# Query loads by one iteration instead of two, and weights issued 600 KB further ahead

## The chip, the cores and the metric

The kernel runs on one core of a Trainium2 chip. The metric is the device time of one execution in microseconds (us). Before the change three runs took 405.43, 406.85 and 407.35 us, median 406.85.

The engines of the core work side by side, each through its own list of instructions in order: TensorE (PE, with its weight loads as PEld), VectorE (DVE), ScalarE (ACT), GpSimd (POOL) and SyncE (SP). They wait for one another through semaphores. SP does nothing here but issue DMA loads and stores, in the order in which the program wrote them; an issue that has to wait holds up all that come after it.

## The reference, cut to what matters

Three steps follow one another: a local attention with global tokens, a soft mixture of experts, and a feed-forward layer.

```
s_g   = scale * q_g @ k_all^T;  out_g = softmax(s_g) @ v_all          # 32 global queries see all keys
s_ll  = where(|i - j| <= 32, scale * q_l @ k_l^T, -1e9)               # 512 local queries: a band
s_lg  = scale * q_l @ k_g^T                                           # and the 32 global keys
out_l = softmax([s_lg, s_ll]) @ [v_g, v_l]
x     = [out_g, out_l], heads side by side                            # 2176 tokens x 512

logits = x @ phi;  d = softmax over tokens;  slots = d^T @ x          # 8 experts x 4 slots
out_e  = relu(slots_e @ w1_e) @ w2_e;  y = softmax over slots(logits) @ out

h = y @ w_in;  g = h - tanh(h);  result = g @ w_out
```

There are 4 batches of 8 heads with 512 local and 32 global positions of 64 numbers, all float32. w1 and w2 are 8 x 512 x 1024 and 8 x 1024 x 512; w_in is 512 x 2048, w_out 2048 x 512. The expert weights are the largest part of the bytes, 33.5 MB.

## The kernel before, in words

**The attention loop** (line 664) makes 33 iterations, `it` = 0 to 32. The 32 pairs of batch and head are taken four at a time, which gives eight *stages* `s`; a stage has four *groups* of queries, `t` = 0 to 3, and iteration `it` = 4s + t scores group `it`. One iteration does several things, each for another group:

- `local_scores(it)` (line 236): PE multiplies the queries with their window of keys (L248), VectorE masks and takes maxima (L254), ScalarE takes the exponentials (L258).
- POOL then prepares the next group: `roll_k(it)` shifts the window of keys in place, and `spread_q(it + 1)` (line 138) copies the next group's queries into `q_b[2]`, the only buffer that the score matmuls read. So this copy waits for the scores of group `it`, and the scores of the next group wait for this copy.
- `local_transpose(it - 1)` (L269), `local_values(it - 2)` (L281) and `global_values(it - 2)` (L475) finish older groups; `roll_v(it - 2)` shifts the values on POOL.
- When `it` % 4 = 2, `global_probs` takes the scores of the next stage's global queries with all of its keys (L430). When t = 1, `spread_k(s + 1)` copies the next stage's global keys beside its local ones, on POOL; when t = 3, `spread_v(s + 1)` does so with global values. In the profile all POOL copies stand at line 210, and are told apart by their tiles: q, k, v, and k<-qg for `spread_k`.

**Where SP's loads come from.** All loads go through `load` (line 98), which adds their KB to the counter `queued` and issues them on SP; in the profile they stand at line 104. In the loop an iteration issues, in this order: queries (in even iterations), the next stage's values (`load_v`, first part with the global values `vg` when t = 2, second part when t = 3), then weights, and, when t = 3, the global queries and keys (`qg`) and the local keys of the stage after the next (`load_qk(s + 2)`).

Queries lie in two buffers `q_b[0]` and `q_b[1]` of 256 KB, each for two groups; group g stands in half g % 2 of buffer (g // 2) % 2. `load_q(h)` in iteration `it` = 2h - 4 fills both halves of buffer h % 2, for groups it + 4 and it + 5. The groups that stood there were it and it + 1, and the last reader of these is `spread_q(it + 1)`, in the same iteration. So SP waits with this load for that copy on POOL.

Weights have no fixed place. The `while` loop of line 724 issues them as long as the KB issued so far are under a pace:

```
while queued < LEAD + PACE * it:
    if len(raw_t) < min(NIN, (it - C0 + 3) // 2 + 1) and free:
        load_raw()
    elif not len(free) > (KEEP if len(raw_t) < NIN else 0) or not load_w():
        break
```

`load_raw` brings 512 KB of w_in as raw words in two loads of 256 KB (`in_w_in`); eight of these are converted during the loop. `load_w` brings one 512 KB piece of w1 or w2 (`in_w`). Both take a slot of 29; a raw slot comes back after its conversion, a weight's slot only when the experts have used it. With LEAD = 2700 and PACE = 1200 the loop may be 2,700 KB ahead of 1,200 KB an iteration. Near the end of the loop, from iteration 27, buffers of the attention are turned into more slots.

**After the loop** come the mixture's slots, the experts (from some 140 us; L971 and L1010), and the feed-forward layer (L1133 and L1174 to L1176), which fills the rest of the time from some 180 us.

Of the kernel before, what the change touches and what calls it, by code (L numbers as in the profile page):

```python
# [18 lines left out]
NT = 17  # L19
NE = 8  # L20
WARM = 3
LEAD, PACE = 2700, 1200
KEEP = 2
SPK = 1
C0 = 4
# [37 lines left out]
def band_attention_soft_moe_tanhshrink_kernel(  # L63
# [34 lines left out]
    def load(out, in_):  # L98
        nonlocal queued
        n = 8 if in_.dtype == mybir.dt.int64 else 4  # L100
        for _, c in out.ap:
            n *= c
        queued += n >> 10
        DMA.dma_start(out=out, in_=in_)  # L104
# [18 lines left out]
    def spread_k(s):  # L123
        kg = qg_t[s][:, 128:192].rearrange("p (i c) -> p i c", i=2)
        pcopy(k_t[s][:, :, 3], kg[:, :, None].to_broadcast([128, 2, 6, 32]))

    def spread_v(s):
        v = v_t[s][96:128]
        pcopy(v[:, 1:6], v[:, 0:1].to_broadcast([32, 5, 260]))


    def load_q(h, cols=slice(0, 256)):
        load(
            out=q_b[h % 2].rearrange("p (a t) -> p a t", a=2)[:, :, cols],
            in_=qd[h // 2][:, :, 256 * (h % 2) + cols.start:256 * (h % 2) + cols.stop],
        )

    def spread_q(g, copies):
        for par in range(2):
            r = slice(64 * par, 64 * par + 64)  # L140
            copies[par](
                q_b[2][r].rearrange("p (a b t) -> p a b t", a=2, b=2)[:, :, par],
                q_b[g // 2 % 2][r].rearrange("p (a h t) -> p a h t", a=2, h=2)[:, :, g % 2],
            )
# [42 lines left out]
    def selectors():  # L187
        V.tensor_reduce(out=istk, in_=ident.rearrange("p (g s) -> p s g", g=4), op=ALU.add, axis=AX.X)
# [13 lines left out]
    NG = 4 * NST  # L202
# [15 lines left out]
    def roll_k(g):  # L218
        k = k_t[g // 4]
        for a, b, q in ROLLS[g % 4]:  # L220
            pcopy(k[:, :, q, a:b], k[:, :, q, a + 1:b + 1])

    def roll_v(g):
        v = v_t[g // 4]
        for a, b, q in ROLLS[g % 4]:
            r = slice(32 * q, 32 * q + 32)
            if g < NG - 2:
                pcopy(v[r, a:b], v[r, a + 1:b + 1])
            else:
                pcopy(v[r, a:b, 0:130], v[r, a + 1:b + 1, 0:130])  # L230
                S.copy(*(v[r, i:i + b - a, 130:260] for i in (a, a + 1)))
# [4 lines left out]
    def local_scores(g, fill):  # L236
        s, t = divmod(g, 4)
        k = k_t[s]
        sm = wk.tile([128, 512], F32, tag="sm", name="sm").rearrange("p (j c) -> p j c", j=4)
        mb = wk.tile([128, 4], F32, tag="mb", name="mb")  # L240
        for f in fill[0:1]:
            f()
        for h2 in range(2):
            sc = psS.tile([128, 2, 128], F32, tag="S", name="sc", padded_shape=[128, 2, 256])
            for a in range(2):
                jj = 2 * h2 + a
                for i in range(2):
                    T.matmul(  # L248
                        sc[64 * i:64 * i + 64, a, :], lhsT=q_b[2][:, 256 * i + jj:256 * i + 256:4],
                        rhs=k[:, i, :, WINDOWS[t][jj][0]], skip_group_check=True, tile_position=(0, 64 * i),  # L250
                    )
            for a in range(2):
                jj = 2 * h2 + a
                V.tensor_tensor_reduce(  # L254
                    out=sm[:, jj, :], in0=sc[:, a, :], in1=mask[WINDOWS[t][jj][1]],
                    scale=-0.125, scalar=3e38, op0=ALU.add, op1=ALU.min, accum_out=mb[:, jj:jj + 1],
                )
                S.activation(  # L258
                    out=sm[:, jj, :], in_=sm[:, jj, :], func=AF.Exp, scale=-1.0, bias=mb[:, jj:jj + 1]
                )  # L260
            for f in fill[1 + h2:2 + h2]:
                f()
        sm_t[g] = sm

    def local_transpose(g):
        p = sm_t.pop(g)
        ps = psT.tile([128, 512], F32, tag="T", name="ptp")
        for u in range(4):
            T.transpose(ps[:, 128 * u:128 * u + 128], p[:, u, :], ident)  # L269
        pt = wk.tile([128, 512], F32, tag="pt", name="pt")  # L270
        S.copy(out=pt, in_=ps)
        pt_t[g] = pt
# [342 lines left out]
    def win_head(c):  # L615
        f32_head(win[c].bitcast(I32), raw_t[c][0])

    def win_ops(c):
        return f32_tail(win[c].bitcast(I32), *raw_t[c])
# [5 lines left out]
    def open_chains():  # L625
        for c in chains:
            if c[0][0]:
                c[0][0]()

    def step_chains():  # L630
        for c in chains:
            if c[0][1]:
                c[0][1]()
        chains[:] = [c[1:] for c in chains if len(c) > 1]
# [5 lines left out]
    with tc.manual_schedule():  # L640
# [23 lines left out]
        for it in range(NG + 1):  # L664
            s, t = divmod(it, 4)
            open_chains()
            last = fill[3:]
            if it < NG:
                local_scores(it, fill)
                if it:  # L670
                    roll_k(it)
                    if it < NG - 1:
                        spread_q(it + 1, (pcopy, pcopy))
            if 1 <= it < NG + 1:
                local_transpose(it - 1)
            free.extend(cool)
            cool.clear()
            if it < NG and it >= C0 and (it - C0) % 2 == 0 and (it - C0) // 2 < NIN:
                win_head((it - C0) // 2)
                fill = win_ops((it - C0) // 2)  # L680
            else:
                fill = []
            if it >= 2:
                local_values(it - 2)
                global_values(it - 2)
                roll_v(it - 2)
            for f in last:
                f()
            step_chains()
            gs = (it + 2) // 4 if it % 4 == 2 and it + 2 < NG else 0 if it == 0 else None  # L690
            if gs is not None:
                c = global_probs(gs)
                c[0][1]()
                if it == 0:
                    spread_q(1, (pcopy, pcopy))
                    roll_k(0)

                chains.append([(c[1][0], c[2][1])] + c[3:] if gs == 0 else c[1:])
            if it == 4:
                selectors()  # L700
            if it % 8 == 7:
                chains.append(global_turn(it // 8))
            i = it - 2
            if i >= 0 and (i // 4) % 2 == 1:
                chains.append(turn_x(4 * (i // 8) + i % 4))
            if it in (11, 19, 27):
                chains.append(dispatch((it - 11) // 8)[0])
            if it < NG and t == SPK and s < NST - 1:
                spread_k(s + 1)
            if it == 0:  # L710
                spread_v(0)
            if it < NG and t == 3 and s < NST - 1:
                spread_v(s + 1)
            if it % 2 == 0 and it < NG - 4:
                load_q(it // 2 + 2)
            if it < NG:
                if it == NG - 5:
                    phi_g = ap_.tile([128, 192], F32, tag="qg", name="phi_g", bufs=1)
                    phi_g = phi_g[:, 0:128].rearrange("p (k s) -> p k s", k=4)
                    load(out=phi_g, in_=phid[1])  # L720
                if t in (2, 3) and 1 <= s < NST - 1:
                    load_v(s + 1, t - 2)
# [6 lines that stand above are left out]
            if it < NG and t == 3 and s + 2 < NST:  # L729
                load_qk(s + 2)  # L730
            if it == NG - 5 or it == NG - 1:
                reuse(ap_.tile([128, 1536], F32, tag="k", name="k_w"))
            if it == NG - 3:
                reuse(ap_.tile([128, 1560], F32, tag="v", name="v_w"))
            if it == NG - 2:
                free.append((wk, "x", 1024, 3))
            if NG - 3 <= it < NG:
                reuse(q_b[it - NG + 3])
            if it == NG - 3:
                reuse(pg[:, 0, 0:512])  # L740
            if it == NG - 1:
                reuse(pg.rearrange("p a c -> p (a c)")[:, 512:1536])
# [676 lines left out]
    with tc.If(small < 1):  # L1419
        for t0, nt in [(0, 4), (4, 2), (6, 4), (10, 2), (12, 3), (15, 2)]:  # L1420
            steps[:] = [(t0, nt, fc, fc == 0, fc == 15) for fc in range(16)]
            for i in range(18):
                if i < 16:
# [3 lines left out]
                    u, g = (r[:, i % 2, 0:n] for r in (u_r, g_r))  # L1427
# [76 lines left out]
```

## Time and profile before

| | us |
|---|---|
| median of 3 runs | 406.85 (405.43 to 407.35) |
| profiled execution, its own time | 406.85 |
| its span, first to last instruction | 405.1 |
| PE busy | 382.9 |
| DVE busy | 276.2 |
| ACT busy | 218.2 |
| POOL busy | 209.7 |

The span is the time between the first and the last instruction; the execution's own time is 1.75 us longer. The profile's page gives each engine's busy time and cuts the span into 40 slices, each with a digit for its busy tenths. Further views list waits (who waited for whom, and how long), give the busy time of stretches, show a timeline of one engine, and list each DMA issue with its KB and the time from its issue to the landing of its last byte. "issue" as the releaser means that the profile shows nothing that was waited for. `sc`, `gsc` and `X` are the tiles of the local scores, the global scores and the local values.

### The profile page before, as it was taken

To read this page: it belongs to the slowest core of one execution; us is meant where nothing else is said; L and a number is where in the kernel's file an instruction comes from. 1 tells how busy PE (TensorE), PEld (TensorE's weight loads), DVE (VectorE), ACT (ScalarE), POOL (GpSimd) and SP (SyncE) were. 2 spreads that over 40 slices of the span, in tenths; PEclk is the share of its full clock that TensorE was granted. 3 is DMA by queue.
4 is the path that set the end of the run, shared out by engine and by line. 5 is a ranking of instruction groups with operands and counts; after the bars stand their busy time and mean duration, and the time that the engine had idled before them with its cause. 6 is when DMAs were issued, how large, how long until landed. Compare 5 with 4: busy or idle time off the path is not lost.

```text
span 405.1 us, 10230 instructions
## 1 busy us (share of the span) xinstructions
PE 382.9 (95%) x3767; PEld 279.6 (69%) x3767; DVE 276.2 (68%) x833; ACT 218.2 (54%) x542; POOL 209.7 (52%) x275
## 2 busy tenths in 40 slices
PE   7889889989999899999999999999989999999994
PEld 3677667766787433336877786786868888888873
DVE  4577698766476526449998886787879997555541
ACT  2677666865766202248655645566575645345330
POOL 3676576665564010016866444455575668347441
PEclk9999999999999999999999999999999999999998
DMA  6899999999768989999303101003100003002104
GB/s 182 264 401 317 321 335 268 357 334 294 266 183 270 332 254 418 416 420 385 111 0 105 53 1 53 0 4 94 60 2 2 0 28 129 0 2 113 44 2 138
DMA packets 33834, 70.43 MB, mean 174 GB/s; under 512 B 3824, under 2 KB 10736, under 8 KB 33776
## 3 DMA queue, kind: packets, MB, share of 16 engines
q1 hardware_dynamic: 33632, 69.56, 50.3%
q8 instruction: 32, 0.52, 0.5%
q14 instruction: 26, 0.21, 0.2%
q10 hardware_dynamic: 144, 0.13, 0.1%
HBM read 65.22 MB, written 4.46 MB: 172 GB/s over the span
## 4 chain that ended last, share of the span: by engine, by line
PE 76%; issue 6%; POOL 5%; DVE 4%; DMA 3%; ACT 3%; SPq 2%; DVEq 0%; POOLq 0%
PE a L1175 13%; PE a L1176 13%; PE a L1174 13%; PE sc L248 7%; PE a L971 4%; PE a L1010 4%; PE h L1133 4%; PE X L281 3%; PE ptp L269 3%; SPq L104 2%; PE gsc L430 2%; POOL q L210 2%; PE xTp L311 2%; PE ps L344 1%; DVE slot L1150 1%
## 5 line engine op out<-in xcount | busy, mean ns | idle before, releaser
L1161 POOL TENSOR_TENSOR slot<-slot 128x384 fp32r<-128x384 f32 x96 | 98.7, 1031 | 83.5 <-ACT slot L1157 79.8
L1174 PE MATMUL a<-slot 128*128 128x512 f32 x272 | 106.9, 393 | 1.3 <-ACT v_w L1182 0.7
L1176 PE MATMUL a<-slot 128*128 128x512 f32 x272 | 107.8, 396 | 0.0
L1175 PE MATMUL a<-slot 128*128 128x512 f32 x272 | 107.5, 395 | 0.0
L1146 DVE SCALAR_TENSOR_TENSOR h<-slot,h 128x384 f32<-128x384 f32 x96 | 51.5, 537 | 38.7 <-ACT slot L1140 38.4
L1157 ACT CAST slot<-slot 128x384 fp32r<-128x384 f32 x96 | 47.6, 496 | 49.5 <-DVE slot L1150 49.0
L1140 ACT ACTIVATE slot<-h 128x384 f32<-128x384 f32 x96 | 45.3, 473 | 34.5 <-PE h L1133 33.9
L1174 PEld LDWEIGHTS a<-slot 128*128 128x128 f32 x272 | 51.1, 188 | 14.2 <-ACT v_w L1182 1.5
L1176 PEld LDWEIGHTS a<-slot 128*128 128x128 f32 x272 | 51.0, 188 | 11.4
L1175 PEld LDWEIGHTS a<-slot 128*128 128x128 f32 x272 | 51.0, 188 | 9.3 <-POOL slot L1037 1.0
L1150 DVE TENSOR_TENSOR slot<-slot,h 128x384 f32<-128x384 f32 x96 | 50.8, 529 | 8.0 <-DVE h L1146 0.5
L258 ACT ACTIVATE sm<-sm,mb 128x128 f32<-128x128 f32 x128 | 41.2, 396 | 15.5 <-DVE mb L254 15.2
L248 PE MATMUL sc<-k,q 128*64 128x128 f32 x512 | 39.0, 294 | 4.9 <-POOL q L210 3.8
L210 POOL TENSOR_SCALAR v<-v 32x1300 f32<-32x1300 f32 (+5 forms) x40 | 34.2, 855 | 13.9 <-PE xgp L475 11.4
L248 PEld LDWEIGHTS sc<-k,q 128*64 128x64 f32 x512 | 33.3, 208 | 11.1 <-POOL q L210 5.9
L210 POOL TENSOR_SCALAR q<-q 64x256 f32<-64x256 f32 x62 | 27.5, 444 | 20.5 <-issue 11.0
L254 DVE CUSTOM_DVE_ANT_0 sm<-sc,mask 128x128 f32<-128x128 f32 x128 | 30.2, 284 | 10.9 <-PE sc L248 9.7
L1037 POOL TENSOR_TENSOR slot<-k_w,slot 128x512 fp32r<-128x512 f32 x16 | 20.7, 1296 | 32.5 <-ACT slot L1036 32.3
L1133 PE MATMUL h<-slot 128*128 128x384 f32 x96 | 32.4, 339 | 0.8 <-DVE slot L1150 0.6
L1133 PEld LDWEIGHTS h<-slot 128*128 128x128 f32 x96 | 17.9, 188 | 12.0 <-DVE slot L1150 5.9
L281 PE MATMUL X<-v,pt 128*32 128x65 f32 x1024 | 22.1, 223 | 1.4 <-issue 1.4
L281 PEld LDWEIGHTS X<-v,pt 128*32 128x32 f32 x1024 | 16.5, 109 | 7.2 <-issue 6.1
(239 smaller groups left out, 526.2 us busy)
## 6 DMA issues: line engine op xcount, KB each, us to landing
slot<-in_w_dram SPq DMA_DIRECT2D x55, 512.0 KB, 7.6
slot<-in_w_out_dram SPq DMA_DIRECT2D x9, 512.0 KB, 4.8
slot<-in_w_in_dram SPq DMA_DIRECT2D x16, 256.0 KB, 6.5
k<-in_k_dram SPq DMA_DIRECT2D x7, 576.0 KB, 7.8
q<-in_q_dram SPq DMA_DIRECT2D x15, 256.0 KB, 5.4
out_dram<-o SPq DMA_DIRECT2D x15, 256.0 KB, 2.1
slot<-in_w_in_dram SPq DMA_DIRECT2D x7, 512.0 KB, 10.0
v<-in_v_dram SPq DMA_DIRECT2D x8, 390.0 KB, 5.5
```

Source lines behind the costliest of these rows:

```text
L210: G.tensor_scalar(out=o, in0=i, scalar1=0.0, scalar2=1.0, op0=ALU.add, op1=ALU.mult)
L248: T.matmul(sc[64 * i:64 * i + 64, a, :], lhsT=q_b[2][:, 256 * i + jj:256 * i + 256:4], rhs=k[:, i, :, WINDOWS[t][jj][0]], skip_group_check ...
L281: T.matmul(X[32 * jj:32 * jj + 32, h, :], lhsT=pt[:, 128 * jj + 32 * h:128 * jj + 32 * h + 32], rhs=v[:, WINDOWS[t][jj][0], 65 * h:65 * h ...
L1133: T.matmul(h, lhsT=mst(128 * fc, 128), rhs=cst(128 * t0 + c.start, n))
L1140: S.activation(out=u, in_=h, func=AF.Square)
L1146: V.scalar_tensor_tensor(out=h, in0=u, scalar=-2.5, in1=h, op0=ALU.add, op1=ALU.mult)
L1150: V.tensor_tensor(out=g, in0=u, in1=h, op=ALU.mult)
L1157: S.copy(out=ghi, in_=g)
L1161: G.tensor_tensor(out=glo, in0=g, in1=ghi.bitcast(F32), op=ALU.subtract)
L1174: T.matmul(acc_t[j], lhsT=ghi[:, c], rhs=whi[fc], start=first, stop=False)
L1175: T.matmul(acc_t[j], lhsT=ghi[:, c], rhs=wlo[fc], start=False, stop=False)
L1176: T.matmul(acc_t[j], lhsT=glo[:, c], rhs=whi[fc], start=False, stop=last)
```

## The change

Query loads now fill half a buffer, for one group. Iteration 0 loads groups 4 and 5; every later iteration loads group it + 5, into the half from which `spread_q(it + 1)` of the same iteration has just copied. Each load has 128 KB instead of 256, there are twice as many, and odd iterations have one, too. LEAD becomes 3300, so that the `while` loop may be 600 KB further ahead.

```
-LEAD, PACE = 2700, 1200
+LEAD, PACE = 3300, 1200
...
-            if it % 2 == 0 and it < NG - 4:
-                load_q(it // 2 + 2)
+            for g in (4, 5) if it == 0 else (it + 5,):
+                if g < NG:
+                    load_q(g // 2, slice(128 * (g % 2), 128 * (g % 2) + 128))
```

`load_q` itself had the second argument before; it was used for the very first queries. The loads ahead of the loop are unchanged.

## Rows read from the trace of the kernel before

**Rows 1.** The page: busy us, share, instructions; DMA tenths; DMA queues.

```profile
PE 382.9 (95%) x3767; PEld 279.6 (69%) x3767; DVE 276.2 (68%) x833; ACT 218.2 (54%) x542; POOL 209.7 (52%) x275
...
DMA  6899999999768989999303101003100003002104
...
q8 instruction: 32, 0.52, 0.5%
```

**Rows 2.** Stretches: length, engines' busy us, PE clock, DMA share, GB/s.

```profile
13.00:110.00 97.00, 88.17 (x1877) 69.44 (x1878) 67.73 (x347) 67.17 (x188) 62.73 (x115) 1.00 0.98 324
110.00:131.00 21.00, 20.78 (x476) 16.29 (x474) 13.94 (x79) 14.19 (x40) 11.66 (x22) 1.00 0.72 216
131.00:180.00 49.00, 47.02 (x410) 18.78 (x409) 23.12 (x89) 11.44 (x40) 3.69 (x4) 0.97 0.97 365
```

**Rows 3.** DMA issues, us to landing, at 4.58, 5.04, 21.31, 21.99, 36.55, 39.18, 109.94.

```profile
v<-in_v_dram SPq DMA_DIRECT2D x1, 390.0 KB, 4.4
q<-in_q_dram SPq DMA_DIRECT2D x1, 128.0 KB, 4.3
qg<-in_qg_dram SPq DMA_DIRECT2D x1, 96.0 KB, 7.2
k<-in_k_dram SPq DMA_DIRECT2D x1, 576.0 KB, 8.0
k<-in_k_dram SPq DMA_DIRECT2D x1, 576.0 KB, 7.8
q<-in_q_dram SPq DMA_DIRECT2D x1, 256.0 KB, 5.9
v<-in_vg_dram SPq DMA_DIRECT2D x1, 32.5 KB, 2.6
```

**Rows 4.** Waits: total us, times, longest; the last from SP's own.

```profile
POOL q L210 <- issue: 11.0, 5, 3.1
ACT L216 <- DMA q<-in_q_dram: 5.9, 1, 5.9
POOL k L210 <- DMA qg<-in_qg_dram: 4.4, 4, 2.2
...
SPq L104 <- POOL q L210: 41.3, 14, 4.8
```

**Rows 5.** Timeline (start, us, instruction) of PE and POOL, 48 to 50.

```profile
48.19 1.19 PE L248 MATMUL sc<-k,q 128*64 128x128 f32 x16
49.52 0.94 POOL L210 TENSOR_SCALAR q<-q 64x256 f32<-64x256 f32 x2 [3.14 <-issue]
```

**Rows 6.** Timeline of SP, POOL and PE around stage 2's keys.

```profile
21.99 0.55 SPq L104 DMA_DIRECT2D k<-in_k_dram  x1
28.68 0.51 POOL L210 TENSOR_SCALAR k<-qg 128x384 f32<-128x384 f32 x1 [1.08 <-DMA qg<-in_qg_dram]
30.45 1.26 PE L430 MATMUL gsc<-k,qg 128*64 128x480 f32 x12
```

**Rows 7.** Timeline of SP at the end of the loop's weights.

```profile
103.20 1.21 SPq L104 DMA_DIRECT2D slot<-in_w_dram  x2
...
112.69 0.55 SPq L104 DMA_DIRECT2D k_w<-in_w_dram  x1
```

**Rows 8.** Timeline of POOL and PE at two copies of global values.

```profile
36.19 1.63 POOL L210 TENSOR_SCALAR v<-v 32x1300 f32<-32x1300 f32 x1 [0.20 <-DMA v<-in_v_dram]
...
67.76 1.27 POOL L210 TENSOR_SCALAR v<-v 32x1300 f32<-32x1300 f32 x1
70.73 1.23 PE L248 MATMUL sc<-k,q 128*64 128x128 f32 x16 [0.39 <-POOL q L210]
```

**Rows 9.** The DMA issue at 61.88: us to landing.

```profile
v<-in_vg_dram SPq DMA_DIRECT2D x1, 32.5 KB, 5.1
```

**Rows 10.** Timeline of PE: first and last of seven gaps.

```profile
20.83 0.32 PE L475 MATMUL xgp<-v,pg 128*32 128x65 f32 x7 [0.30 <-issue]
...
106.31 0.33 PE L460 MATMUL gtp<-ident,pg 128*128 128x128 f32 x1 [0.69 <-issue]
```

## The prediction

> **What bounds the kernel now.** I read the page first [rows 1]: 382.9 of 405.1 us have TensorE (PE) busy, and the DMA row shows nines over much of the first half, then almost nothing. The change touches only what the sync engine (SP) issues in the attention loop, so the next view is the busy time by stretch [rows 2]. From 13 to 110 us the DMA engines are at 0.98 of their time at 324 GB/s, PE at 88.17 of 97.00 us. From 110 to 131 us DMA falls to 0.72; from 131 to 180 us (the experts) it is back at 0.97. So while the loop runs the DMA queue is full, and a load's landing time is set by how many KB stand ahead of it, not by when it was issued. The issue rows confirm it: loads of 96 and 576 KB land 7.2 and 8.0 us after issue [rows 3], while a 32.5 KB load late in the loop, with little ahead of it, needs 2.6 us [rows 3].
>
> Third, the waits [rows 4]. What waits for a query load? Once, ScalarE at the start, 5.9 us, on a load that is not changed. GpSimd (POOL) before its query copies sat 11.0 us until "issue", five times, the longest 3.1. The timeline shows what that is [rows 5]: the copy starts at 49.52, and PE's score matmuls run 48.19 to 49.38. The copy overwrites the buffer that these matmuls read; it starts 0.14 us after them. It is a wait for PE, not for a load. So no query load after the first is late: **there is no stall for earlier queries to remove.** What does wait for DMA in the loop: POOL for the global queries and keys (qg), 4.4 us in four, and little else [rows 4].
>
> **The change part by part.**
>
> *Queries by single iterations.* Fourteen loads of 256 KB (one stands in [rows 3]) become 28 of 128 KB. For an odd group nothing moves (iteration g-5 is the even one in which its pair was loaded); for an even group the load comes one iteration earlier. Gain: none, by the paragraph above. Costs:
> (a) Fourteen more issues on SP at about 0.55 us [rows 6], 7.7 us. SP spends 41.3 us waiting for POOL's query copies [rows 4]; that hides them.
> (b) DMA time. The unchanged 128 KB load, issued at 5.04, landed 4.3 later at 9.3, the load ahead of it at 4.58 + 4.4 = 9.0: 0.4 us of queue time. A 256 KB one landed at 39.18 + 5.9 = 45.1, behind keys at 36.55 + 7.8 = 44.35: 0.7 us [rows 3]. A pair costs 2 x 0.4 - 0.7 = 0.1 us more. Bounds: 0 (half the KB, half the time) to 0.7 (a small load costs what a large one does). I take 0.15, by the nearest row, since 0.4 is rounded down.
> (c) In odd iterations SP now waits for POOL's copy of that iteration; before, it issued that iteration's loads right behind the even one's. Queued behind this wait are the second part of the values, raw weights, expert weights, and the next-but-one stage's qg and keys. They go out up to one iteration (97 us for some 25 iterations, 3.9 us) later. The full queue covers that: 7.2 us from issue to landing against 2.6 at least leaves 4.6 us of standing in line. If the queue ran dry the cover is gone and up to 3.9 us per stage could show.
>
> *LEAD 3,300.* The units are KB. I counted the loop of line 724 through all iterations with the sizes of the issue rows; for before, the count gives exactly the order of SP's rows. Up to and including stage 2's keys (iteration 3): before 3,154 ahead of the loop + 256 + 512 + 256 + 1,024 + 512 + 1,024 + 672 = 7,410. After: 3,154 + 256; + 128 + 512 + 512; + 128 + 1,024; + 128 + 512 + 1,024 + 672 = 8,050. That is one 512 KB weight load and one 128 KB query load more ahead of the keys. At most other places it is also 512 or 640 KB more, at stage 3's keys 128, at stage 2's global values none. Does the earlier weight help anything? Both versions fill the 29 slots, before by iteration 25, after by 24, and then stop: in the rows two weight loads at 103.20 are the last ones until a key buffer is freed at 112.69 [rows 7]. The experts begin with the same weights on chip; gain 0.
>
> *What the KB cost.* A weight load costs 1.4 us of queue: 524,288 bytes at the 365 GB/s of the experts' stretch, where the queue carries little else [rows 2]. Stage 2's keys: 1.4 + 0.4 + two pairs x 0.15 = 2.1 us later. They landed at 21.99 + 8.0 = 30.0 [rows 3, 6]; PE reads them at 30.45 [rows 6], with no idle time before: 0.4 us of slack. **PE stalls 2.1 - 0.4 = 1.7 us at the global scores of stage 2.** qg (21.31 + 7.2 = 28.5) slips alike; POOL already waited 1.08 for it [rows 6], and its copies still end before the delayed scores do.
>
> After that PE is late by 1.7 and slack has grown by as much. Stage 2's global values (same KB ahead, four pairs, +0.6) cost nothing more and give 0.2 back: POOL waited 0.20 for them at 36.19 [rows 8]. Stage 4's: 1.4 + 8 x 0.15 = 2.6 later than 61.88 + 5.1 = 67.0 [rows 9], so 69.6; POOL copied them from 67.76, now from 67.76 + 1.5 = 69.3; 0.3 more, and this place counts, as PE waited 0.39 for POOL right behind it at 70.73 [rows 8]. The other stages, counted the same way, have more room. Sum 1.7 - 0.2 + 0.3 = **+1.8 us** at the loop's end. The experts start later by that: their loads wait for slots that PE frees, so it passes on.
>
> The profiled execution took 406.85 us (span 405.1 and 1.75 around it), which is also the median of the three runs. 406.85 + 1.8 gives 408.6.
>
> **Rivals.**
>
> *Small loads cost what large ones do, and the keys are late in every stage (slower).* Place: the DMA queue in the loop. Price: 0.7 more per pair. Stage 2's keys 1.4 + 0.7 + 1.4 - 0.4 = 3.1; stage 4's global values 1.4 + 8 x 0.7 - 0.7 = 6.3, the largest lateness, so about 413. It decides from 0.2 us per pair on: there stage 4's values alone make 1.4 + 1.6 - 0.7 = 2.3 us, over the bound of 0.5% below. Against it: the 128 KB row says 0.4. For it: that is a single row, read to 0.1, and the price I take, 0.15, is close to the 0.2.
> The Trainium skill, "DMA: Bandwidth & Descriptors", section "Bandwidth", says to batch transfers to at least 1 MiB and lists 0.95 us for 64 KB and 6.15 us for 1 MB. A straight line between these is an estimate of 1.3 us for 128 KB and 2.0 for 256 KB: 0.6 more per pair, and a time near 413 by it. The trace disagrees at its 128 KB row, 0.4 us.
>
> *The queue is smoother and PE's own stalls shrink (faster).* PE has seven gaps until "issue" in the middle of a run of equal matmuls, from 0.30 at 20.83 to 0.69 at 106.31, 5.6 us in sum [rows 10]; instructions come through the same DMA engines, 32 packets for 0.52 MB [rows 1]. Bursts of ten loads, as every fourth iteration issues now, become halves. If half of the gaps went and the keys came in time: 406.85 - 2.8 = 404.0. Against it: the DMA share would stay at 0.98, with more KB waiting.
> The same page, section "Queues, rings and completion order", has every DMA engine take turns between its queues packet by packet. By it a fetch waits for a packet or so, however long the other queue is, and the gaps would stay; no row here separates the two.
>
> *Nothing moves.* The extra KB are absorbed, because DMA stretches that were slow for their own reasons aren't slow again, or the keys' 2.1 us prove 1. Price 0 to 0.5: 406.9. For it: only 1.7 us stand between slack and none. Against it: 640 KB at 324 GB/s are 2.0 us by the stretch's rate too.
>
> **How the numbers follow.** A measurement of this kernel can tell 0.5% (2.0 us) from no change: 404.8 to 408.9 is "same". Forecast, 407.3 to 410.0: chance 0.46, of which 0.15 lies above 408.9. Nothing moves: 0.20. Slower rival, 410 to 413: 0.18. Faster rival: 0.16, of which 0.13 lies below 404.8. So faster 0.13, slower 0.15 + 0.18 = 0.33, same 0.54. Range 404.5 to 411.5: it leaves out about 0.11 below and 0.07 above.
>
> **What would show it.** Right: PE idle ahead of stage 2's global scores (L430, near 32), their keys landing near 32.0; a DMA share near 1 from 13 to 110 us; the experts starting 1 to 3 us later; the same time from there to the end. Wrong in the size: pairs that cost more than 0.2 us. Wrong in kind: PE starting the global scores at 30.5 as now, a DMA queue that runs empty in odd iterations, or PE's "issue" gaps changing by more than 2 us.

## The result, and the profile after

The changed kernel took 408.43 us (median of 20 runs, 405.76 to 412.36), the kernel before 405.87 in 20 runs (402.51 to 408.58): a ratio of 1.0071 [1.0042, 1.0100]. A second comparison gave 1.003 [0.9991, 1.0069], which doesn't tell the change from none. Ratios leave out the executions that the record counts as slow, medians don't, so the two can differ by some 0.1%. The prediction was 408.6. The profiled execution of the changed kernel took 407.04 us, 1.4 below its median, and that of before 406.85, 1.0 above its own. So the two spans, 405.3 and 405.1, differ by far less than the medians, and one pair of traces doesn't show where the time went. Both kernels were therefore run and profiled again, and two versions with the same loops beside them. That gives three traces of either loop, which I use together below.

The page after, against [rows 1], and the busy time by stretch against [rows 2]:

```profile
PE 382.0 (94%) x3767; PEld 279.6 (69%) x3767; DVE 275.2 (68%) x833; ACT 219.6 (54%) x542; POOL 208.4 (51%) x275
...
PEclk9998999999999999999999999999999999999998
DMA  7999999999967999999303101003100003002104
```

```profile
13.00:110.00 97.00, 87.05 (x1810) 68.43 (x1810) 65.71 (x341) 66.51 (x184) 60.46 (x112) 0.98 1.03 321
110.00:131.00 21.00, 20.78 (x505) 16.42 (x504) 13.69 (x81) 14.69 (x43) 12.20 (x25) 1.00 0.69 203
131.00:180.00 49.00, 46.98 (x446) 19.78 (x448) 23.86 (x95) 12.30 (x42) 4.43 (x6) 1.00 0.99 371
```

TensorE (PE) was busy 1.1 us less from 13 to 110 us, the DMA queue as full as before. The granted clock is the other difference: 0.98 instead of 1.00 in this stretch. Next PE's waits in the loop, from 8 to 130 us (what waits <- for what: total us, times, longest):

```profile
PE sc L248 <- POOL q L210: 6.7, 9, 1.4
PE gsc L430 <- DMA k<-in_k_dram: 2.0, 1, 2.0
PE gtp L452 <- issue: 0.9, 1, 0.9
PE xgp L475 <- issue: 0.8, 1, 0.8
PE ptp L269 <- ACT pt L271: 0.7, 3, 0.2
```

The second row is new: before, PE never waited for keys. The timeline shows it at stage 2, at the place of [rows 6]; then the DMA issues from 21 to 26 us, the keys' at 24.87 among them, against [rows 3]:

```profile
24.87 0.54 SPq L104 DMA_DIRECT2D k<-in_k_dram  x1
...
31.79 0.51 POOL L210 TENSOR_SCALAR k<-qg 128x384 f32<-128x384 f32 x1 [3.91 <-DMA qg<-in_qg_dram]
...
33.21 1.89 PE L430 MATMUL gsc<-k,qg 128*64 128x480 f32 x12 [2.04 <-DMA k<-in_k_dram]
...
34.88 1.93 PE L248 MATMUL sc<-k,q 128*64 128x128 f32 x16
```

```profile
k<-in_k_dram SPq DMA_DIRECT2D x1, 576.0 KB, 8.3
...
q<-in_q_dram SPq DMA_DIRECT2D x2, 128.0 KB, 6.6
```

The keys are issued 2.9 us later than before and land at 24.87 + 8.3 = 33.2 instead of 30.0. The global scores start at 33.21 instead of 30.45, and take 1.89 us instead of 1.26. The reason for the second figure stands in the clock column of a finer table of stretches:

```profile
30.00:33.70 3.70, 1.66 (x70) 1.19 (x70) 0.84 (x5) 1.62 (x4) 1.76 (x5) 0.99 1.07 383
33.70:37.10 3.40, 3.40 (x30) 2.51 (x27) 2.03 (x11) 1.06 (x4) 1.03 (x2) 0.50 0.80 239
```

Right behind the wait PE ran at 1.2 instead of 2.4 GHz for 3.4 us; half of that, 1.7 us, is an estimate of the work lost. Over the wait and the fall PE's scores went from 0.3 us behind those of before (27.93 against 27.66) to 3.5 (38.88 against 35.36). In the trace of before the clock doesn't fall inside the loop; its first fall is at 140.1 us.

Where the loop's time goes, over three traces of either loop: the start of the last iteration's scores lay at 124.70, 124.64 and 122.20 us with the old loads, at 126.32, 126.06 and 124.06 with the changed ones, **1.6, 1.4 and 1.9 us later**. All PE's idle time from 8 to 130 us, each gap over 0.15 us counted, was 9.8, 8.6 and 7.8 before, 11.1, 10.6 and 10.4 after: 2.0 more on the mean.

### The profile page after: what moved, and what is told of

Its sections match the earlier page's. It is cut to its first block, busy times and chain, and to the rows that moved or that the text cites. A ratio compares the mean times of both kernels' runs of the same rounds, so it can differ in the third digit from the quotient of the medians.

```text
span 405.3 us, 10259 instructions
## 1 busy us (share of the span) xinstructions
PE 382.0 (94%) x3767; PEld 279.6 (69%) x3767; DVE 275.2 (68%) x833; ACT 219.6 (54%) x542; POOL 208.4 (51%) x275
## 4 chain that ended last, share of the span: by engine, by line
PE 72%; POOL 7%; DMA 6%; issue 5%; DVE 4%; ACT 3%; SPq 1%; DVEq 0%; POOLq 0%; ACTq 0%
PE a L1177 13%; PE a L1176 13%; PE a L1175 13%; PE sc L248 6%; PE a L1011 4%; PE a L972 4%; PE h L1134 3%; PE ptp L269 3%; PE X L281 3%; POOL slot L1162 2%; DMA k<-in_k_dram 2%; POOL v L210 2%; PE gsc L430 2%; DMA v<-in_v_dram 2%; POOL q L210 2%
## 5 line engine op out<-in xcount | busy, mean ns | idle before, releaser
L248 PE MATMUL sc<-k,q 128*64 128x128 f32 x512 | 40.0, 299 | 7.6 <-POOL q L210 6.7
L1038 POOL TENSOR_TENSOR slot<-k_w,slot 128x512 fp32r<-128x512 f32 x16 | 20.7, 1295 | 32.8 <-DMA slot<-in_w_dram 24.8
L269 PE MATMUL ptp<-ident,sm 128*128 128x128 f32 x128 | 21.1, 288 | 0.8 <-ACT pt L271 0.7
```

The lines of the kernel that those rows point to most:

```text
L248: T.matmul(sc[64 * i:64 * i + 64, a, :], lhsT=q_b[2][:, 256 * i + jj:256 * i + 256:4], rhs=k[:, i, :, WINDOWS[t][jj][0]], skip_group_check ...
```

## The experiments

Ratios are against runs of the kernel before on the same chip, with 95% intervals. **Theory**: the additional KB ahead of stage 2's keys make them late, and little else counts. **Rival**: the cost lies elsewhere, in the form of the loads or in many places.

### The two parts alone

`e1_split`, the changed kernel with the old lead:

```diff
-LEAD, PACE = 3300, 1200
+LEAD, PACE = 2700, 1200
```

> The changed kernel with LEAD back at 2,700: only the split of the query loads is left. By the count of the loop, 384 KB less than before stand ahead of stage 2's keys, 128 more at the later keys. Theory KB (what stands ahead of the keys decides): stage 2's keys land by 30 us, PE doesn't wait for them (gap before the global scores of stage 2 under 0.3 us), time 405 to 406.5, within 0.3% of before. Rival SPLIT (twice as many loads and a wait for POOL in every iteration are the price): the time stays 2 to 3 us over before, near 408.4, whatever the keys do. Rival CLOCK (only the fall of TensorE's clock after the wait costs): as KB, no fall inside the attention loop.

`e2_lead`, the kernel before with the new lead:

```diff
-LEAD, PACE = 2700, 1200
+LEAD, PACE = 3300, 1200
```

> The kernel before with LEAD 3,300: only the earlier weights. 512 KB more than before stand ahead of stage 2's keys and 1,024 ahead of stage 3's. Theory KB: those keys land 1.3 us later or more, at 31.3 to 32.5; PE waits 0.8 to 2 us ahead of stage 2's global scores; time 1 to 3 us over before, 407 to 409. Rival SPLIT: the keys' lateness costs nothing in the end, time 405 to 406.5.

Measured: 1.0022 [0.9986, 1.0059] for the queries alone (407.35 us against 406.20), 1.0047 [1.0005, 1.0089] for the lead alone (407.41). The two add up to 1.0069, near the 1.0071 of the whole change; with these intervals, and with 1.003 in the second comparison, that proves nothing. The time of e1_split is over its expected 405 to 406.5. PE's row at stage 2's global scores, of e1_split and then of e2_lead:

```profile
30.59 1.26 PE L430 MATMUL gsc<-k,qg 128*64 128x480 f32 x12
```

```profile
32.11 1.26 PE L430 MATMUL gsc<-k,qg 128*64 128x480 f32 x12 [1.27 <-DMA k<-in_k_dram]
```

The wait comes with the lead alone (keys at 31.98) and is gone without it (29.65), as expected of the two. But the last iteration's scores start at 124.24 us in e2_lead and at 123.39 in e1_split, within the 122.20 to 124.70 of the three traces with the old loads. So these traces show what the lead does to the keys, and not that this wait is what it costs.

### Two cures for the keys

`e3_latelead`, the changed kernel with the new lead only behind iteration 3:

```diff
-            while queued < LEAD + PACE * it:
+            while queued < (LEAD if it > 3 else 2700) + PACE * it:
```

> The changed kernel, but with 3,300 only from iteration 4 on and 2,700 up to iteration 3: 384 KB less than before ahead of stage 2's keys, all later stages as in the changed kernel (the same KB from iteration 4 on). Theory KB with stage 2 as the one place: PE doesn't wait at stage 2's global scores, and the time is at most 0.8 us over before (405.5 to 406.7), 2 us or more under the changed kernel. If the later stages' lateness (global queries waited for in seven places, 13.1 us) costs as much: 407 to 408.5. Rival SPLIT: 408.4.

`e4_keysfirst`, the changed kernel with the keys' loads of the stages ahead of the weights of the same iteration:

```diff
+            if it < NG and t == 3 and s + 2 < NST:
+                load_qk(s + 2)
             while queued < LEAD + PACE * it:
...
-            if it < NG and t == 3 and s + 2 < NST:
-                load_qk(s + 2)
```

> The changed kernel with one thing moved: in the iterations with t = 3 the global queries and keys are issued ahead of that iteration's weights instead of behind them. In iteration 3 that takes 1,536 KB from in front of stage 2's keys, in the others 512 to 1,024. Theory KB: the keys land 3 us or more earlier in every stage, POOL's wait for global queries falls from 13.1 us to under 3, no wait of PE for keys, time 404 to 406, at or under before. Rival SPLIT: the waits go and the time stays at 408.

Both expectations failed: 1.0078 [1.0040, 1.0116] and 1.0073 [1.0041, 1.0106], 409.81 and 409.13 us. The cures did what they should at the keys: PE waited 0.34 and 0.00 us there. The timelines at 38 to 42 us show what came in its place, in e3_latelead and then in e4_keysfirst:

```profile
39.10 1.27 POOL L210 TENSOR_SCALAR v<-v 32x1300 f32<-32x1300 f32 x1 [2.23 <-DMA v<-in_vg_dram]
...
41.76 1.23 PE L248 MATMUL sc<-k,q 128*64 128x128 f32 x16 [1.98 <-POOL q L210]
```

```profile
38.27 1.27 POOL L210 TENSOR_SCALAR v<-v 32x1300 f32<-32x1300 f32 x1 [2.62 <-DMA v<-in_vg_dram]
...
40.92 1.99 PE L248 MATMUL sc<-k,q 128*64 128x128 f32 x16 [2.61 <-POOL q L210]
```

GpSimd (POOL) copies the stage's global values and behind them the queries that PE waits for. The global values are the next load in the line, and the weights that were taken from in front of the keys stood in front of these: by the count, as many KB as in the changed kernel. They landed at 38.96 and 38.12, against 37.32, 38.21 and 37.49 in its three traces. In [rows 8] POOL waited 0.20 us at this place; but in c1_before_again (below), the kernel before unchanged, POOL waited 1.40 and PE 1.29 us there. In e3_latelead and e4_keysfirst the clock then fell to 1.2 GHz for 3.4 us, at 43.2 and at 41.0. So the keys' wait was taken away and the cost was not. How much of the wait that came in its place is the edit's doing, one trace of each can't tell, and their executions (410.89 and 412.24 us) took 1.1 and 3.1 us more than the medians.

### A smaller lead

`e5_before2100`, the kernel before, and `e6_split1500`, the changed one:

```diff
-LEAD, PACE = 2700, 1200
+LEAD, PACE = 2100, 1200
```

> The kernel before with LEAD 2,100: 1,024 KB less than before ahead of the keys and values of stages 2 and 3, 512 less later; the 29 slots are still full by iteration 25. Theory KB (the loop loses what its keys, global queries and global values come late): POOL no longer waits for either (before: 4.4 us for global queries), time 403.5 to 405.3, under before by 0.5 to 2 us. Rival SPLIT-AND-WAIT (in the changed kernel the splitting alone costs, the KB nothing): same as before, 405.4 to 406.4. Rival CLOCK (only falls of TensorE's clock differ): as before, with as much time at the lower clock.

```diff
-LEAD, PACE = 3300, 1200
+LEAD, PACE = 1500, 1200
```

> The changed kernel with LEAD 1,500: query loads split as there, but 900 to 1,500 KB less than before ahead of every stage's keys and values; slots full by iteration 27. Theory KB: the waits for keys, global queries and global values go although the loads are split: time 403.5 to 406, 2.5 us or more under the changed kernel. Rival SPLIT-AND-WAIT: 407 or more, as the split with 2,700 (407.2 mean against 405.8 of before).

Both failed: 1.0036 [1.0004, 1.0068] and 1.0061 [1.0019, 1.0103], 407.69 and 409.27 us. The time of e6_split1500 is the one expected of its rival, that splitting costs by itself; but e5_before2100, without the split, was slower too. In e5_before2100 (traced execution 410.46 us) PE's gaps in the loop came to 8.5 us, as with the old loads, and it still ended late, its last scores at 127.17. Its timeline of PE shows two waits, and its stretches the clock behind them:

```profile
7.83 1.52 PE L248 MATMUL sc<-k,q 128*64 128x128 f32 x16 [1.91 <-ACT q L216]
...
56.02 0.62 PE L452 MATMUL gtp<-ident,pg 128*128 128x128 f32 x3 [2.04 <-issue]
```

```profile
8.00:12.00 4.00, 4.00 (x37) 3.00 (x38) 1.84 (x10) 1.39 (x4) 1.61 (x4) 0.57 0.41 128
...
56.40:59.80 3.40, 3.40 (x48) 2.76 (x48) 0.52 (x3) 1.20 (x4) 0.70 (x2) 0.50 1.05 384
```

Two waits of about 2 us, one at the start-up and one "until issue", and behind each of them the clock at half: neither is, by the profile, a wait for a load that the lead moves. In e6_split1500 the global values of stage 2 landed at 38.24 (old loop: 36.05, 38.22 and 36.30) although by my count 1,536 KB fewer stood ahead of them, and PE waited 2.14 us at 41.04. The stretch from 13 to 40 us, of before and then of e6_split1500:

```profile
13.00:40.00 27.00, 24.35 (x517) 19.35 (x519) 18.03 (x96) 19.49 (x53) 18.40 (x34) 1.00 1.02 346
```

```profile
13.00:40.00 27.00, 24.02 (x510) 18.88 (x509) 18.03 (x98) 20.23 (x58) 17.43 (x33) 1.00 0.96 278
```

The DMA engines are busy for 0.96 of the time and deliver 278 GB/s; before, 346 at 1.02. A full queue has no fixed rate, so counted KB give a landing time only while the mix of loads stays as it was. What sets the rate stays open.

### The price of a small load

`e7_two_small`, the kernel before with each pair's load cut in two, one right behind the other in the program:

```diff
-                load_q(it // 2 + 2)
+                load_q(it // 2 + 2, slice(0, 128))
+                load_q(it // 2 + 2, slice(128, 256))
```

> The kernel before with each query load issued as two of 128 KB one right after the other, in the same places and with the same KB counts: only the size of the loads changes. By the prediction's price of 0.15 us of queue a pair: 2 us of queue by iteration 26, global values of stage 4 some 1.2 us later, time 405.8 to 407 (0 to 1.2 over before). If a small load costs what a large one does (0.7 a pair): 409 or more. If size costs nothing: 405.4 to 406.2.

`e8_qlast`, the changed kernel with the query load as the last of its iteration:

```diff
-            for g in (4, 5) if it == 0 else (it + 5,):
-                ...
...
                 load_qk(s + 2)
+            for g in (4, 5) if it == 0 else (it + 5,):
+                ...
```

> The changed kernel with the query load issued as the last load of its iteration instead of the first: values, weights, global queries and keys no longer stand behind SP's wait for POOL's copy of the same iteration, and one query load of 128 KB less stands ahead of them; loads, sizes and KB per iteration are the same. Rival WAIT (the wait on POOL in odd iterations delays the others' issue): time falls to 406 to 407, 1.5 us or more under the changed kernel. Theory KB (the landing is set by the KB ahead in a full queue, not by the time of issue): 407.5 to 409, within 1 us of the changed kernel.

e7_two_small took 408.88 us, 1.0064 [1.0035, 1.0093]: a miss, and next to the 409 of a small load that costs what a large one does. In the changed kernel's queue the price was as put, though. Where a query load follows another load's landing, it does so 0.40 us later (median of 23 loads of 128 KB in the changed kernel's loop) against 0.70 (12 of 256 KB before), so a pair costs 0.1 us there; with the 0.90 of c1_before_again (below, 12 loads of 256 KB) it would cost nothing. In e7_two_small itself the second half waits for POOL's copy (issues at 46.44 and 48.62, for one), and it landed 0.40 to 1.11 us behind the first in the seven cases on record. Its price is not settled by that. The keys landed late:

```profile
33.55 1.26 PE L430 MATMUL gsc<-k,qg 128*64 128x480 f32 x12 [1.57 <-DMA k<-in_k_dram]
```

They landed at 33.41 us, later than in any trace of the changed loop, with as many KB ahead of them as before: the count of KB alone doesn't set a landing.

e8_qlast took 412.72 us (six runs), 1.0160 [1.0113, 1.0206], which no theory had. In its trace one "issue" wait of 1.97 us at 83.74 stands ahead of a fall of the clock; but the traced execution, 408.88 us, is the shortest of the six and doesn't show where the rest went. Why the order of one small load costs that much is open.

### Both again, and with the clock's help

`c1_before_again` and `c2_after_again` are the two kernels unchanged. `f1_before_fill` and `f2_after_fill` are the two with three more matmuls whose results nothing reads, at places where PE would idle: behind the warm-up, and ahead of lines 856 and 890.

```diff
+        T.matmul(warm[:, 0:256], lhsT=ones, rhs=ones[:, None, :].to_broadcast([128, 2, 128]), skip_group_check=True)
...
+        keep_warm(mp[:, 256:512], 256)
...
+        keep_warm(bank(0), 256)
```

> The kernel before, unchanged, run like a variant. All eight variants so far came out slower than before. If the comparison is fair: ratio 1.000 within 0.4%, 405.4 to 406.6, and a second trace that shows how far the landings of the loop differ between two executions of one program. If whatever is run as the variant comes out slower: 407 or more, and the results so far say less.

> The changed kernel, unchanged, for a second trace and a second measure: 407.5 to 409.5. Theory LATE (later landings make PE wait, and a wait of some 2 us is followed by 3.4 us of TensorE at half clock): again more of PE's waits for POOL and DMA in the loop than the 3.8 us of before, and more time at the lower clock than before in the mean over the runs. Rival CHANCE (the first trace's wait for stage 2's keys was an accident of that execution): waits as in before, no more time at the lower clock.

> The kernel before with three matmuls that compute nothing that is used, of 256 columns each: one behind the warm-up ahead of the loop, two in the short waits between the loop and the experts (before PE's waits of 0.44 and 0.69 us). The clock fell at these two places in several traces, for 3.4 or 6.8 us. If filling the waits keeps the clock up: no fall near 8 and near 140 us, mean clock 0.995 or more, time 403.5 to 405.3, under before by 0.5 to 2. If not: 405.5 to 407, the matmuls' own time (0.5 us each) added.

> The changed kernel with the same three matmuls. They touch nothing inside the loop. Theory LATE puts the change's cost inside the loop (waits and falls of the clock there): the distance to the filled kernel before stays 2 to 3.5 us, time 406 to 408. Rival ELSEWHERE (the change costs because the start and the experts fall to the lower clock more often): the distance shrinks under 1.5 us.

Measured against one pool of runs: 0.9988 [0.9949, 1.0027], 1.0030 [0.9991, 1.0069], 0.9971 [0.9928, 1.0014] and 1.0007 [0.9966, 1.0048]. The first shows the comparison to be fair to 0.5%. f1_before_fill kept the clock up as expected (mean 0.995), but its 406.15 us are over the expected 403.5 to 405.3. The change costs 1.2 us here by medians without the filler (408.08 less 406.92) and 0.9 with it (407.05 less 406.15); by means of the runs in the ratios, 1.6 and 1.7. The expectation of f2_after_fill had 2 to 3.5 us for a cost inside the loop and under 1.5 for one at the start and the experts. The distance with the filler speaks rather for the second, but it was no larger without it, so this test decides nothing. PE's waits in the loop of c1, c2, f1 and f2 in turn, the rows of POOL's query copies and of the global scores, and one more for f2:

```profile
PE sc L248 <- POOL q L210: 4.1, 8, 1.3
...
PE gsc L430 <- DMA k<-in_k_dram: 0.6, 1, 0.6
```

```profile
PE sc L248 <- POOL q L210: 5.7, 8, 1.2
PE gsc L430 <- DMA k<-in_k_dram: 2.0, 1, 2.0
```

```profile
PE sc L248 <- POOL q L210: 4.7, 9, 1.0
PE gsc L430 <- issue: 1.5, 1, 1.5
```

```profile
PE sc L248 <- POOL q L210: 5.5, 8, 1.0
PE X L281 <- issue: 2.3, 3, 1.4
PE gsc L430 <- DMA k<-in_k_dram: 1.2, 1, 1.2
```

The wait for stage 2's keys is there in every trace of the changed loop and, but for 0.6 us, in none of the old one. Neither c2's nor f2's was followed by a fall of the clock. f1's trace, 403.4 us, has no fall but at its end. It has the lowest ratio of all versions, but its interval reaches over 1, so I don't call it faster than the kernel before.

## Why the prediction was right, step by step

**No query load was late, so nothing to gain.** Right: no run with the split queries was faster, and e1_split, the split alone, is at 1.0022.

**A pair costs 0.15 us.** Measured 0.1 or less in the changed loop, by the landings above, and the time is far from the small-load rival's 413; e7_two_small's own landings leave a higher price open for its order of issue. The weight load's 1.4 us were a little too much: the experts' weights land 1.24 us apart in a row. By the table of the Trainium skill, "DMA: Bandwidth & Descriptors", section "Bandwidth", which is for loads that GpSimd issues, a pair would cost 0.6 us more, an estimate; in this queue, where many loads stand in line, the changed kernel's trace doesn't follow it.

**The keys 2.1 us later, and PE 1.7 us idle ahead of them.** Right in place, and in size on the mean of three traces. They landed at 30.0, 31.8 and 30.0 us in the three traces of the old loop (mean 30.6), at 33.2, 33.1 and 32.0 in the changed one (32.8): 2.2 later. PE's wait was 2.04, 1.97 and 1.22, 1.7 on the mean, against 0, 0.55 and 0. One profile each would have given 3.1 for the landing: a single trace is a poor measure of one load. What I did not have is that this landing differs by 1.8 us between two executions of the same kernel (c1 against before), and that other things than KB move it: 33.4 in e7_two_small with no KB more, 31.3 in e3_latelead with 384 fewer. That the KB ahead made the keys late is argued, not shown.

**+0.3 at stage 4's global values.** I put the landing at 69.6; it was 70.3, and POOL waited:

```profile
55.57 1.27 POOL L210 TENSOR_SCALAR v<-v 32x1300 f32<-32x1300 f32 x1 [1.11 <-DMA v<-in_vg_dram]
...
70.43 1.78 POOL L210 TENSOR_SCALAR v<-v 32x1300 f32<-32x1300 f32 x1 [0.33 <-DMA v<-in_vg_dram]
```

PE's next scores fell from 2.4 to 2.9 us behind those of before. The size is about right; in the other two pairs these values landed 3.6 and 0.6 us later.

**"The other stages have more room."** Wrong in extent. The first row of the fence is stage 3's global values, and for the global queries POOL waited 10.7, 11.7 and 11.5 us in the changed loop, six times, against 2.2, 4.6 and 1.8. From stage 2 on, the copies start 0.14 us behind their landing nearly everywhere: the slack is used up. Most of these waits lie beside PE's work, but PE's wait for POOL's query copies grew from a mean of 4.2 to 6.0 us, where the sum had 0.1. The dearest place is stage 6's global values. They landed at 102.7 us instead of 96.4, and PE waited behind POOL:

```profile
102.80 1.27 POOL L210 TENSOR_SCALAR v<-v 32x1300 f32<-32x1300 f32 x1 [2.76 <-DMA v<-in_v_dram]
```

```profile
105.46 1.23 PE L248 MATMUL sc<-k,q 128*64 128x128 f32 x16 [1.44 <-POOL q L210]
```

In c2 PE waited 1.06 us there, in f2 and in the old loop not at all.

**The faster rival.** It had PE's "issue" gaps shrink, and they did on the mean, from 3.8 to 1.9 us, but they differ by execution (5.6, 3.0, 2.7 before; 1.7, 1.0, 3.0 after), and other runs with split loads had 1.6 to 5.8. So no effect of the change on them is shown. The prediction named a change of over 2 us as a sign of being wrong in kind: the first pair shows 3.9 less, the others 2.0 less and 0.3 more. What PE waits for in these gaps, the traces do show. All 52 of them over 0.3 us, in the loops of all fourteen traces, end 1.2 to 1.7 us behind the end of an instruction packet of 16 KB on DMA queue q8, where one comes every 6 us or so; the ends of PE's other gaps lie anywhere from 0.1 to 9.2 us behind one. The packet from 83.77 to 85.08 us in the kernel before, and PE's gap up to 86.53:

```profile
q8 instruction: 1, 0.02, 5.8%
```

```profile
86.53 0.74 PE L344 MATMUL ps<-xT,phi 128*32 128x128 f32 x18 [1.38 <-issue]
```

So PE waited there for instructions, as the rival supposed (that q8 carries PE's is concluded from these times); why some packets come too late and most don't stays open. The rule of turns between queues that the prediction took from the Trainium skill, "DMA: Bandwidth & Descriptors", section "Queues, rings and completion order", is neither borne out nor refuted by that.

**+1.8 at the loop's end.** Measured 1.6, 1.4 and 1.9, but partly by luck. On the mean PE's waits grew by 1.6 us at stage 2's keys and by 1.8 at POOL's query copies, the "issue" gaps gave back 1.9, and the first pair has a fall of the clock on top: two terms of nearly two us that the sum had at 0.1 and at nothing cancelled. Nor did the lateness stay once it was there: in the first pair it was 3.3 us behind the keys (scores at 34.88 against 31.54), 0.2 at 96.28 against 96.09, and 1.6 at the end. That 408.6 met 408.43 so closely is luck as well: the 406.85 that it starts from lies 1.0 over the median of 20 runs, and the first comparison's 2.6 us lie 0.8 over the forecast 1.8.

**"It passes on."** Right by the medians (2.6 and 1.2 us), not in each execution, and not for the reason I gave. From about 150 us the experts' weights land one per 1.24 us, and at 175 PE has caught up with them: the stage ends with the last landing. SP's 21 weight issues of this stage in the changed kernel and, behind it, in the kernel before:

```profile
136.44 23.66 SPq L104 DMA_DIRECT2D slot<-in_w_dram  x21
```

```profile
134.81 25.29 SPq L104 DMA_DIRECT2D slot<-in_w_dram  x21
```

They start 1.6 us apart and end together at 160.1. Two things took the difference away. In the kernel before the clock fell at 140.1, as PE began with the weights whose slots these loads refill, and the changed kernel had no such fall. In c1 and f1 a hole of 1.5 us came into the landings, behind 169.5 and 166.2 us, though the DMA moved as many bytes as in the kernel before (417 GB/s from 165 to 177 us in c1). The issue to landing of the stage's last weight in c1, and then in c2:

```profile
slot<-in_w_dram SPq DMA_DIRECT2D x1, 512.0 KB, 11.4
```

```profile
slot<-in_w_dram SPq DMA_DIRECT2D x1, 512.0 KB, 9.9
```

PE waits for the last ones in c1:

```profile
175.98 1.05 PE L1010 MATMUL a<-slot 128*32 128x512 f32 x4 [0.19 <-DMA slot<-in_w_dram]
177.22 1.05 PE L1010 MATMUL a<-slot 128*32 128x512 f32 x4 [0.19 <-DMA slot<-in_w_dram]
```

So at the last of these weights the three pairs of traces are 0.4, -0.6 and 1.7 us apart; in the third the clock fell at 140.2 us in f2 and not in f1. Why the medians of the first comparison differ by more than the loop (2.6) isn't isolated. Part of it may be the clock, but that isn't shown: its mean was 0.9889 over the changed kernel's first runs, with none on record for the kernel before beside them. In the second comparison it was 0.9912, against 0.9924 in c1 and 0.9911 in the pool of the kernel before, so no difference there.

## What to carry to other kernels

In a full DMA queue, count the KB ahead of each load that something waits for, and price an edit at the load with the least slack: here that gave the place, and the mean lateness of these keys. Don't take the count for the cause, or for a cure. Keys with no KB more ahead landed later still (e7_two_small), what moves behind the first load stands ahead of the second, and the rate isn't fixed. And a sum that comes out isn't a mechanism shown: here terms that it left out cancelled. All eight other orders and leads tried came out 0.2 to 1.6% above the kernel before, the least of them within its interval, so compare several traces and many runs before a single wait is blamed.

## What the runs showed of the hardware

- A wait of PE can cost more than its length: the changed kernel's wait of 2.04 us put PE 3.2 us further behind, the fall of the clock behind it included. All falls of the clock inside the loop in these traces stood right behind one wait of 1.9 to 2.6 us, of whatever cause (keys, POOL, "issue", start-up), and each held PE at 1.2 GHz for 3.4 us. But c2's wait of 1.97 us, f2's of 1.22 and e7's of 1.57 for the same keys had none: in c2 the global scores took 1.26 us, in the changed kernel's first trace 1.89.
- The share of busy time of the DMA engines doesn't tell what they deliver: 346, 315 and 278 GB/s from 13 to 40 us at 1.02, 0.99 and 0.96 (before, after, e6_split1500).
- SP never had more than eight loads under way. In none of the fourteen traces was a load issued while more than seven earlier ones were on record as not yet landed, and seven was the commonest number: 48 of 158 issues up to 180 us in the kernel before, 58 of 171 in the changed one. SP then waits for a landing: from 12 to 112 us 2.6, 7.2 and 2.0 us of such waits with the old loads, 9.1, 9.7 and 7.7 with the changed ones. A limit that counts loads and not KB would fit; no run here tests it, and the prediction's count leaves it out.
- PE's "issue" gaps in the loop go with its instruction packets: all 52 over 0.3 us ended 1.2 to 1.7 us behind the end of one, and came to 1.0 to 5.8 us a trace.
- Executions of one kernel differ by 6 us and more (402.5 to 408.6 for the kernel before). Early loads do too: stage 1's keys landed at 14.8 us in its first trace and at 17.2 in c1, though the loop's last scores started at 124.7 and 124.6.
